# Thresholds on POOL in two batches, first-chunk casts on ACT, and one copy for the last columns of two tiles

## The chip, the cores and the metric

The kernel runs on one core of one Trainium2 chip. The metric is the device time of one execution in microseconds (us), the median of three runs. One execution was also taken by the hardware profiler; its trace is what the tables below are read from. The engines are PE (matrix multiply; PEld is its weight load), DVE (vector), ACT (activation, with function tables), POOL (GpSimd) and SP, which only issues DMAs here.

## What is computed

Eight batches of eight heads of attention over 576 positions of 64 values, with a threshold: a score counts only if it is at least the row's maximum minus tau. The result goes through a feed-forward layer with softplus.

```python
scores = scale * np.matmul(q, k.transpose(0, 1, 3, 2))
thresh = np.max(scores, axis=-1, keepdims=True) - tau
scores = np.where(scores >= thresh, scores, -1000000000.0)
attn = np.exp(scores - np.max(scores, axis=-1, keepdims=True))
attn = attn / (np.sum(attn, axis=-1, keepdims=True) + 1e-09)
attn_out = np.matmul(attn, v)
...
h = x @ w_in
g = np.maximum(h, 0.0) + np.log1p(np.exp(-np.abs(h)))
return (g @ w_out).astype(np.float32)
```

Here x is the attention output as 4608 rows of 512, w_in is 512 x 2048 and w_out 2048 x 512.

## The kernel before

**Attention.** Two heads of a batch form a unit; there are 32 units, four to a batch. A unit has nine tiles of 128 query rows: tiles 0 to 3 are of the first head, tiles 5 to 8 of the second, and tile 4 holds the last 64 rows of both. The 288 tiles run in order. For each tile, `scores` (L375) multiplies on PE into one of two PSUM banks (s_0, s_1), `row_max` (L395) takes the negated row maximum on DVE (L398, negm) and makes the threshold thr from it, `exps` (L405) takes the exponential on ACT (L406), and `mask` (L409) multiplies the exponentials by "score at least thr" on DVE (L411), which also gives the row sums. `weights_T` (L428) transposes the masked tile on PE in pieces of 128 columns (L444), and the last 64 columns of two neighbouring tiles together as one piece (L441); a tile 4 has a piece of its own (L447).

**Upper and lower parts.** PE multiplies in fp32r, a rounded form. So each operand is split into an upper part (a cast) and a lower part (the value minus its upper part). For the attention weights `weights_hi` (L468) copies the transposed pieces on ACT into gH (L464 in batch 0, where signs are turned, L466 elsewhere), and `weights_lo` (L476) makes the lower parts (by PE in batch 0, L485 and L487; by DVE elsewhere, L125). The lower parts of the last 64 columns (L497, L500 through L125) are put in the other 64 partitions of the same columns of gH. `values` (L502) multiplies with v and `values_out` (L515) puts the result into xp. `scale_x` (L550) scales xp on POOL by row factors that come back by DMA, and it goes to DRAM.

**The thresholds.** In batch 0 (the first TG = 36 tiles) thr is made by ACT (L400), in all later tiles by DVE (L402):

```python
nc.vector.reduce_max(negm, s.sp[t][:, :, 0:HS], axis=AX.XY, negate=True)
if 9 * NPAIR * s.b + 9 * s.hp + t < TG:
    nc.scalar.activation(thr, negm, AF.Identity, bias=ntau, scale=-1.0)
else:
    nc.vector.tensor_scalar(out=thr, in0=negm, scalar1=-1.0, scalar2=ntau, op0=ALU.mult, op1=ALU.add)
```

**Feed-forward.** Rows of x go in nine chunks of 512. `hidden` (L590) multiplies with w_in (L603, L605, L607), `softplus` (L618) runs on ACT over two PSUM banks at a time, with a load of its function table, and `parts_of` (L635) splits each result st: the upper part by DVE (L122, GV = 1), the lower by POOL (L125). `project` (L652) multiplies with w_out (L661 to L665). Chunk 0 starts at tile 41, in batch 1, and its matmuls are dealt out among the tiles.

**The weights.** The two weight matrices come as 64-bit words and are made into fp32 upper and lower parts while batches 0 and 1 run, in 32 pieces, one every two tiles: ACT (L176), POOL (L177), DVE three times (L181, L182, L184), POOL twice (L118, L125), and for w_in a store to DRAM and a load back.

**What sets the order.** The program is written out tile by tile by a loop over step letters (L888). A scheduler then places the instructions on each engine by the priority of their place in the program and by when it reckons them ready, so the order on an engine is not the written one, and it changes when a step moves to another engine. Each engine runs its instructions in the order it was given.

Of the kernel before, what the change touches and what calls it, by code (L numbers as in the profile page):

```python
# [12 lines left out]
AF = mybir.ActivationFunctionType  # L13
ALU = mybir.AluOpType
# [9 lines left out]
P = 128  # L24
# [26 lines left out]
GV = 1  # L51
TG = 36
W1 = 2.0
W0 = 1
SPA = 0


@with_exitstack
def tile_kernel(ctx: ExitStack, tc: tile.TileContext, q, k, v, tau, w_in, w_out, out):
# [8 lines left out]
    nc = tc.nc  # L68
# [6 lines left out]
    NC = SM // P  # L75
    NPAIR = H // 2
# [25 lines left out]
    ntau = cpool.tile([P, 1], F32, name="ntau")  # L102
# [4 lines left out]
                            op0=ALU.is_ge, op1=ALU.mult)  # L107
# [8 lines left out]
    def hi_of(eng, out_, in_):  # L116
        if eng is nc.gpsimd:
            eng.tensor_scalar(out=out_, in0=in_, scalar1=1.0, scalar2=1.0, op0=ALU.mult, op1=ALU.mult)  # L118
        elif eng is nc.scalar:
            eng.copy(out_, in_)  # L120
        else:
            eng.tensor_copy(out_, in_)  # L122

    def lo_of(eng, out_, in_, hi):
        eng.tensor_tensor(out=out_, in0=in_, in1=hi.bitcast(F32), op=ALU.subtract)  # L125
# [123 lines left out]
    for b in range(B):  # L249
        for kind in (("one", "two") if b < NSPLIT else ("all",)):  # L250
            for hp in range(NPAIR):
                s = Unit()
# [12 lines left out]
                s.cols = (slice(0, NC), slice(0, 2), slice(2, NC))[("all", "one", "two").index(kind)]  # L265
                s.eng = (nc.gpsimd, nc.scalar)[SPA] if b < NSPLIT else nc.gpsimd
                s.neg = 9 * NPAIR * b + 9 * hp < TG
# [127 lines left out]
    def row_max(s, t):  # L395
        negm = apool.tile([P, 1], F32, tag="negm", bufs=3, name=f"negm_{s.i}_{t}")
        thr = apool.tile([P, 1], F32, tag="thr", bufs=3, name=f"thr_{s.i}_{t}")
        nc.vector.reduce_max(negm, s.sp[t][:, :, 0:HS], axis=AX.XY, negate=True)  # L398
        if 9 * NPAIR * s.b + 9 * s.hp + t < TG:
            nc.scalar.activation(thr, negm, AF.Identity, bias=ntau, scale=-1.0)  # L400
        else:
            nc.vector.tensor_scalar(out=thr, in0=negm, scalar1=-1.0, scalar2=ntau, op0=ALU.mult, op1=ALU.add)  # L402
        s.m[t] = (negm, thr)
# [10 lines left out]
    def group(s, g):  # L414
        if g not in s.grp:
            h = apool.tile([P, NC + 1, 320], F32R, tag="gH", name=f"gH_{s.i}_{g}")
            l = apool.tile([P, NC, 320], F32R, tag="gL", name=f"gL_{s.i}_{g}")
            s.grp[g] = (h, l)
        return s.grp[g]

    def mate(s, t):

        if t == NC:
            return None, False
        u = t if t < NC else t - 1
        return (t + 1, False) if u % 2 == 0 else (t - 1, True)
# [23 lines left out]
    def rests(s, t):  # L450

        lo, hi = slice(0, SR), slice(SR, P)
        other, second = mate(s, t)
        if other is None:
            return [(t, lo, lo, hi)]
        if not second:
            return []
        return [(x, (lo, hi)[s.half[x]], (lo, hi)[s.half[x]], (hi, lo)[s.half[x]]) for x in (other, t)]
# [3 lines left out]
    def copy(s, out_, in_):  # L462
        if s.neg:
            nc.scalar.activation(out_, in_, AF.Copy, scale=-1.0)  # L464
        else:
            nc.scalar.copy(out_, in_)  # L466

    def weights_hi(s, t):  # L468
        main, rest = s.sp[t]
        for g, c0, s0, n in s.place[t]:  # L470
            copy(s, group(s, g)[0][:, 0:NC, c0:c0 + n], main[:, :, s0:s0 + n])
        for x, rows, up, _ in rests(s, t):
            for g, c0, s0, n in s.place[x]:
                copy(s, group(s, g)[0][up, NC, c0:c0 + n], rest[rows, s0:s0 + n])

# [142 lines left out]
    def softplus(u, full):  # L618


        ts, last_ = [], None
        with tc.high_priority(SPP):
            for fc, bank in reversed(full):
                t = fpool.tile([P, TC], F32, tag="st", bufs=NST, name=f"st_{u.n}_{fc}")
                i = nc.scalar.activation(t, bank, AF.Softplus).ins  # L625
                if last_ is not None:
                    tc.add_manual_dep(i, last_.name, mybir.DependencyInfo(
                        mybir.DependencyClass.NoSync, mybir.DependencyReason.DATA), reason="one table load")
                last_ = i
                ts.append((fc, t))  # L630
        defer(HD[1], lambda: [parts_of(u, fc, t) for fc, t in reversed(ts)])
# [3 lines left out]
    def parts_of(u, fc, t):  # L635

        pool, tags, bufs = (fpool, ("gh", "gl"), NG)
        if u.tail:
            spare = [("kT", 2), ("qT0", 2), ("qT1", 2), ("nat", 3), ("vt", 3)]
            i = later_g[0] % (NG + len(spare))  # L640
            later_g[0] += 1
            if i >= NG:
                tag, bufs = spare[i - NG]
                pool, tags = apool, (tag, tag)
        gh, gl = [pool.tile([P, TC], F32R, tag=tags[i], bufs=bufs, name=f"g{i}_{u.n}_{fc}") for i in range(2)]
        hi_of(nc.vector if GV else nc.scalar, gh, t)
        lo_of(nc.gpsimd, gl, t, gh)
        for i in range(TC // u.T):
            c = slice(i * u.T, (i + 1) * u.T)
            u.g[fc + i] = (gh[:, c], gl[:, c])  # L650
# [118 lines left out]
    while sum(u.T for u in chunks) < NT:  # L769
        u = Chunk()  # L770
# [24 lines left out]
    for kind, g in WL:  # L795
        for m in range(4):
            n = len(prep)
            prep.append((int(W0 + n * W1), prep_w_in if kind == "i" else prep_w_out,
                         (g, m) if kind == "i" else (4 * g + m,)))
# [72 lines left out]
    u0.eng, u0.eng_lo = eng, nc.gpsimd  # L872
    scores(*tiles[0])
    row_max(*tiles[0])
    exps(*tiles[0])
    scores(*tiles[1])
# [5 lines left out]
    for g, (cur, t) in enumerate(tiles):  # L882
# [5 lines left out]
        for step in PAT0 + ("m" if g == TG - 1 else "") if g < TG else PAT:  # L888
            if step == "T":
                weights_T(cur, t)  # L890
            elif step == "h":
                weights_hi(cur, t)
            elif step == "l":
                weights_lo(cur, t)
            elif step == "R" and nxt:
                row_max(*nxt)
            elif step == "e" and nxt:
                exps(*nxt)
            elif step == "m" and nxt:
                mask(*nxt)  # L900
            elif step == "M":
                mask(cur, t)
            elif step == "f":
                upto += quota / PAT.count("f")
                while done < upto:
                    done += next(ffn)
            elif step == "x":
                extras(cur.i, cur.tiles.index(t))
            elif step == "S" and g + 2 < NS:
                scores(*tiles[g + 2])  # L910
            elif step == "w":
                while prep and prep[0][0] <= g:
                    _, f, a = prep.pop(0)
                    f(*a)
            elif step == "p":
                point()
# [38 lines left out]
```

## Time and profile before

| what | value |
|---|---|
| median of three runs | 1489.3 us (1488.03 to 1491.64) |
| the profiled execution | 1491.63 us, of which the span from first to last instruction is 1489.6 us |
| PE | 1416.6 us busy, 95% of the span |
| PE weight load | 1195.5 us, 80% |
| DVE | 1019.5 us, 68% |
| ACT | 892.2 us, 60% |
| POOL | 600.3 us, 40% |
| mean granted clock of PE | 0.986 of full speed |

The page of the profile divides the span into 40 slices of some 37 us. In the first eight PE is busy for 6 to 9 tenths and the others for 4 to 9; from the ninth on PE shows 9 tenths, which here means 90% or more, in every slice but the last. Batch 0 runs to about 157 us, batch 1 to about 325 us. A busy PE is not PE at its peak, since matmuls are pipelined and their ends are modelled.

### The profile page before, as it was taken

Reading aid. Unit: us, or ns where it says so; the run is one execution under the profiler, and the core shown is the slowest. Engines: PE = TensorE matmul, PEld = TensorE weight load, DVE = VectorE, ACT = ScalarE, POOL = GpSimd, SP = SyncE. Lnnn points to the kernel's source line nnn. Section 1 sums busy time; section 2 is a strip of 40 time slices with the busy share of each in tenths; the row PEclk is TensorE's granted clock in tenths of the full one; section 3 lists DMA queues with packets and bytes.
Section 4 is the critical chain, followed back from the end, with each engine's and each line's share of the span. In section 5 each row is a group of like instructions: output and inputs, shape, how many; then the busy total and the mean of one; then the engine's idle time right before and its main releaser. Section 6 shows DMA issues by size and latency. Waiting matters only on the chain.

```text
span 1489.6 us, 23959 instructions
## 1 busy us (share of the span) xinstructions
PE 1416.6 (95%) x8024; PEld 1195.5 (80%) x8024; DVE 1019.5 (68%) x2267; ACT 892.2 (60%) x1783; POOL 600.3 (40%) x629
## 2 busy tenths in 40 slices
PE   6787789899999999999999999999999999999998
PEld 5777667678888888888888888888888888788887
DVE  6878889878777777777777777777777777411111
ACT  5887577556766576666666676667665666411110
POOL 4656565534433443344334443334334331323221
PEclk9999899999999999999999999999999999999999
DMA  6756576434443454335333544345333532343321
GB/s 182 195 152 185 145 218 176 132 99 140 129 119 116 118 157 113 96 103 151 110 106 111 150 118 118 108 133 150 113 111 101 153 99 82 96 148 112 122 92 43
DMA packets 131211, 189.96 MB, mean 128 GB/s; under 512 B 35312, under 2 KB 86800, under 8 KB 131088
## 3 DMA queue, kind: packets, MB, share of 16 engines
q1 hardware_dynamic: 131088, 188.43, 43.9%
q8 instruction: 64, 1.05, 0.3%
q14 instruction: 59, 0.48, 0.1%
HBM read 140.51 MB, written 27.41 MB: 113 GB/s over the span
## 4 chain that ended last, share of the span: by engine, by line
PE 66%; ACT 11%; DVE 10%; issue 5%; POOL 4%; DMA 3%; SPq 1%; POOLq 0%; ACTq 0%; DVEq 0%
PE s L392 8%; PE s L444 7%; PE o L665 7%; PE o L663 7%; PE o L661 6%; PE h L603 6%; PE h L605 6%; PE h L607 6%; PE pv L510 3%; PE pv L511 3%; ACT gH L466 3%; DVE e_all L411 2%; ACT L625 2%; ACT e_all L406 2%; ACT st L625 2%
## 5 line engine op out<-in xcount | busy, mean ns | idle before, releaser
L466 ACT CAST gH<-s 128x512 fp32r<-128x512 f32 (+3 forms) x560 | 207.7, 401 | 142.1 <-PE s L444 135.2
L125 POOL TENSOR_TENSOR g<-st,g 128x512 fp32r<-128x512 f32 x144 | 192.3, 1353 | 188.4 <-DVE g L122 188.4
L411 DVE SCALAR_TENSOR_TENSOR e_all<-s,thr,e_all 128x576 f32<-128x576 f32 x288 | 233.9, 815 | 39.0 <-ACT e_all L406 36.4
L398 DVE TENSOR_REDUCE negm<-s 128x1 f32<-128x576 f32 x288 | 217.2, 754 | 38.2 <-PE s L392 34.4
L665 PE MATMUL o<-wo_o,g 128*128 128x512 f32 x576 | 231.9, 403 | 5.6 <-POOL g L125 5.6
L605 PE MATMUL h<-xl,wi 128*128 128x512 f32 x576 | 233.9, 406 | 0.0
L661 PE MATMUL o<-wo_o,g 128*128 128x512 f32 x576 | 232.8, 404 | 0.0
L603 PE MATMUL h<-xh,wi 128*128 128x512 f32 x576 | 230.8, 401 | 1.5 <-ACT xh L120 0.9
L607 PE MATMUL h<-xh,wi 128*128 128x512 f32 x576 | 230.3, 400 | 0.0
L663 PE MATMUL o<-wo_o,g 128*128 128x512 f32 x576 | 228.6, 397 | 0.0
L406 ACT ACTIVATE e_all<-s,negm 128x576 f32<-128x576 f32 x288 | 214.0, 744 | 20.0 <-DVE negm L398 8.5
L125 DVE TENSOR_TENSOR gL<-s,gH 128x512 fp32r<-128x512 f32 (+1 forms) x280 | 175.0, 633 | 60.8 <-ACT gH L466 54.4
L392 PE MATMUL s<-kT,qT 128*128 128x288 f32 x1024 | 195.7, 313 | 7.9 <-DVE gH L125 3.6
L392 PEld LDWEIGHTS s<-kT,qT 128*128 128x128 f32 x1024 | 151.3, 193 | 25.8 <-DVE gH L125 15.7
L122 DVE CAST g<-st 128x512 fp32r<-128x512 f32 x144 | 67.6, 505 | 147.4 <-ACT st L625 146.7
L444 PE MATMUL s<-identr,e_all 128*128 128x128 f32 x1008 | 158.4, 280 | 9.4 <-DVE e_all L411 8.0
L625 ACT ACTIVATE st<-h 128x512 f32<-128x512 f32 x144 | 78.2, 596 | 118.3 <-PE h L607 117.7
L510 PE MATMUL pv<-gH,vt 128*128 128x320 f32 (+1 forms) x512 | 145.6, 304 | 1.8 <-ACT gH L466 1.8
L511 PE MATMUL pv<-gL,vt 128*128 128x320 f32 (+1 forms) x512 | 143.5, 301 | 0.5 <-DVE gL L125 0.5
L444 PEld LDWEIGHTS s<-identr,e_all 128*128 128x128 f32 x1008 | 114.2, 141 | 34.5 <-DVE e_all L411 30.3
L665 PEld LDWEIGHTS o<-wo_o,g 128*128 128x128 f32 x576 | 108.4, 188 | 30.1 <-POOL g L125 11.7
L603 PEld LDWEIGHTS h<-xh,wi 128*128 128x128 f32 x576 | 108.7, 189 | 24.7 <-ACT xh L120 1.2
(104 smaller groups left out, 2374.3 us busy)
## 6 DMA issues: line engine op xcount, KB each, us to landing
wi<-wi_d SPq DMA_DIRECT2D x144, 512.0 KB
qT<-qT SPq DMA_DIRECT2D x124, 128.0 KB
R<-r_d SPq DMA_DIRECT2D x64, 144.0 KB
kn<-in_k_dram SPq DMA_DIRECT2D x32, 256.0 KB
qn<-in_q_dram SPq DMA_DIRECT2D x32, 256.0 KB
vn<-in_v_dram SPq DMA_DIRECT2D x32, 256.0 KB
wc_i<-in_moe_w_in_dram SPq DMA_DIRECT2D x16, 512.0 KB
wi_d<-wc_i SPq DMA_DIRECT2D x32, 256.0 KB
```

The costliest lines, as they stand in the source:

```text
L125: eng.tensor_tensor(out=out_, in0=in_, in1=hi.bitcast(F32), op=ALU.subtract)
L392: nc.tensor.matmul(sp[:, hf, 0:HS], lhs, s.kT[j][:, k0 + hf * HS:k0 + (hf + 1) * HS], start=(m == 0), stop=(m == len(parts) - 1))
L406: nc.scalar.activation(e_all[:, s.half[t], :].rearrange("p (h n) -> p h n", h=2), s.sp[t][:, :, 0:HS], AF.Exp, bias=s.m[t][0], scale=1.0)
L411: nc.vector.scalar_tensor_tensor(out=e2, in0=s.sp[t][:, :, 0:HS], scalar=s.m.pop(t)[1], in1=e2, op0=ALU.is_ge, op1=ALU.mult, accum_out=s.s ...
L444: nc.tensor.matmul(main[:, c, :], e[:, c0:c0 + P], ident, is_transpose=True, start=True, stop=True)
L466: nc.scalar.copy(out_, in_)
L603: nc.tensor.matmul(h, wi[:, 0, cc, :], u.h[cc], start=(cc == 0), stop=False)
L605: nc.tensor.matmul(h, wi[:, 0, cc, :], u.l[cc], start=False, stop=False)
L607: nc.tensor.matmul(h, wi[:, 1, cc, :], u.h[cc], start=False, stop=(cc == NCC - 1))
L661: nc.tensor.matmul(o, gh[:, sl], wo[fc][:, 0, :], start=(i == 0), stop=False)
L663: nc.tensor.matmul(o, gh[:, sl], wo[fc][:, 1, :], start=False, stop=False)
L665: nc.tensor.matmul(o, gl[:, sl], wo[fc][:, 0, :], start=False, stop=(i == QF - 1))
```

## The change

Three edits. The thresholds of batches 0 and 1 (72 tiles) are made by POOL instead of ACT (batch 0) and DVE (batch 1); later batches keep DVE. The 16 upper parts of chunk 0's softplus results are cast by ACT instead of DVE; later chunks keep DVE. And where the last 64 columns of two neighbouring tiles stand in one transposed piece, one copy of 128 partitions x 256 replaces two copies of 64 partitions x 128: it writes the piece twice, side by side, and the half of each that doesn't belong there is written over by the lower parts, as before. There are four such pairs in a unit, 128 in all.

```diff
+TP = 2
...
-        if 9 * NPAIR * s.b + 9 * s.hp + t < TG:
-            nc.scalar.activation(thr, negm, AF.Identity, bias=ntau, scale=-1.0)
+        if s.b < TP:
+            nc.gpsimd.tensor_scalar(out=thr, in0=negm, scalar1=-1.0, scalar2=ntau, op0=ALU.mult, op1=ALU.add)
         else:
             nc.vector.tensor_scalar(out=thr, in0=negm, scalar1=-1.0, scalar2=ntau, op0=ALU.mult, op1=ALU.add)
...
-        for x, rows, up, _ in rests(s, t):
+        both = rests(s, t)
+        if len(both) == 2:
+
+            (g, c0, _, n), = s.place[both[0][0]]
+            copy(s, group(s, g)[0][:, NC, c0:c0 + 2 * n].rearrange("p (k n) -> p k n", k=2),
+                 rest.unsqueeze(1).to_broadcast([P, 2, n]))
+            return
+        for x, rows, up, _ in both:
...
-        hi_of(nc.vector if GV else nc.scalar, gh, t)
+        hi_of(nc.vector if u.n else nc.scalar, gh, t)
```

The edits also let the scheduler place other instructions differently in batches 0 and 1. In the rows below a name ends in a running number; negm_2_3_1179 is the row maximum of unit 2, tile 3, and wa_o1 is a piece of w_out on its way through the three DVE steps L181, L182 and L184. The line numbers of the changed kernel are higher by one (by eight from L476 on).

DVE in batch 0, from the row maximum of unit 2's tile 2 to its mask and the next, before:

```order
L398 TENSOR_REDUCE negm_2_2_1133<-s_0_137 128x1
L181 TENSOR_SCALAR wa_o1_1170<-wa_o1_1170 128x512
L182 SCALAR_TENSOR_TENSOR wa_o1_1170<-wc_o1_1169,wa_o1_1170 128x512
L522 TENSOR_TENSOR xp_1_766<-xp_1_766,pv_1_3_1116 64x256
L184 SCALAR_TENSOR_TENSOR wa_o1_1170<-wc_o1_1169,wa_o1_1170 128x512
L398 TENSOR_REDUCE negm_2_3_1179<-s_1_138 128x1
L497 SCALAR_TENSOR_TENSOR gH_2_0_1104<-tr_2_1_1139,gH_2_0_1104 64x128 x2
L411 SCALAR_TENSOR_TENSOR e_all_136,sums_2_1002<-s_0_137,thr_2_2_1134,e_all_136 128x576
L411 SCALAR_TENSOR_TENSOR e_all_136,sums_2_1002<-s_1_138,thr_2_3_1180,e_all_136 128x576
```

Before, seven instructions stand between the maximum and the mask of this tile, three of them steps of a weight piece. The same place in the changed kernel:

```order
L399 TENSOR_REDUCE negm_2_2_1125<-s_0_137 128x1
L412 SCALAR_TENSOR_TENSOR e_all_136,sums_2_995<-s_1_138,thr_2_1_1082,e_all_136 128x576
L530 TENSOR_TENSOR xp_1_761<-xp_1_761,pv_1_3_1108 64x256
L412 SCALAR_TENSOR_TENSOR e_all_136,sums_2_995<-s_0_137,thr_2_2_1126,e_all_136 128x576
L505 SCALAR_TENSOR_TENSOR gH_2_0_1096<-tr_2_1_1131,gH_2_0_1096 64x128 x2
L399 TENSOR_REDUCE negm_2_3_1170<-s_1_138 128x1
L182 TENSOR_SCALAR wa_o1_1161<-wa_o1_1161 128x512
L183 SCALAR_TENSOR_TENSOR wa_o1_1161<-wc_o1_1160,wa_o1_1161 128x512
L399 TENSOR_REDUCE negm_2_4_1218<-s_0_137 128x1
L185 SCALAR_TENSOR_TENSOR wa_o1_1161<-wc_o1_1160,wa_o1_1161 128x512
L412 SCALAR_TENSOR_TENSOR e_all_136,sums_2_995<-s_1_138,thr_2_3_1171,e_all_136 128x576
```

Now the mask of tile 2 stands ahead of the weight steps, of the lower parts (L505) and of the next maximum; the mask of tile 3 no longer follows at once. The five places of this kind in batch 0 are tiles 2 and 4 of unit 1, tiles 2 and 7 of unit 2 and tile 4 of unit 3.

POOL in batch 1, around the lower parts of chunk 0's softplus results (g1_0) and the weight pieces wc_i3, before:

```order
L125 TENSOR_TENSOR g1_0_3_2511<-st_0_3_2475,g0_0_3_2510 128x512
L177 TENSOR_SCALAR wa_i3_2_2473<-wa_i3_2_2473 128x512
L118 TENSOR_SCALAR wc_i3_2_2472<-wa_i3_2_2473 128x512
L125 TENSOR_TENSOR wc_i3_2_2472<-wa_i3_2_2473,wc_i3_2_2472 128x512
L125 TENSOR_TENSOR g1_0_4_2648<-st_0_4_2622,g0_0_4_2647 128x512
L125 TENSOR_TENSOR g1_0_5_2652<-st_0_5_2620,g0_0_5_2651 128x512
L177 TENSOR_SCALAR wa_i3_3_2587<-wa_i3_3_2587 128x512
L551 TENSOR_TENSOR xp_4_2062<-xp_4_2062,R_4_2538 128x576
```

And in the changed kernel:

```order
L126 TENSOR_TENSOR g1_0_3_2490<-st_0_3_2455,g0_0_3_2489 128x512
L119 TENSOR_SCALAR wc_i3_2_2452<-wa_i3_2_2453 128x512
L126 TENSOR_TENSOR wc_i3_2_2452<-wa_i3_2_2453,wc_i3_2_2452 128x512
L401 TENSOR_SCALAR thr_5_2_2469<-negm_5_2_2468,ntau_85 128x1
L178 TENSOR_SCALAR wa_i3_3_2566<-wa_i3_3_2566 128x512
L401 TENSOR_SCALAR thr_5_3_2528<-negm_5_3_2527,ntau_85 128x1
L126 TENSOR_TENSOR g1_0_4_2626<-st_0_4_2600,g0_0_4_2625 128x512
L559 TENSOR_TENSOR xp_4_2045<-xp_4_2045,R_4_2517 128x576
L126 TENSOR_TENSOR g1_0_5_2630<-st_0_5_2598,g0_0_5_2629 128x512
L178 TENSOR_SCALAR wa_o8_2692<-wa_o8_2692 128x512
L119 TENSOR_SCALAR wc_i3_3_2565<-wa_i3_3_2566 128x512
L126 TENSOR_TENSOR wc_i3_3_2565<-wa_i3_3_2566,wc_i3_3_2565 128x512
```

A threshold now stands behind whatever POOL has ahead of it: thr_5_2 behind the two steps of a weight piece, thr_5_4 (the next row after these) behind two more.

## Rows read from the trace of the kernel before

**Rows 1.** Stages: PE, PEld, DVE, ACT, POOL busy us (instructions), granted clock, DMA.

```profile
10.00:160.00 150.00, 117.55 (x757) 104.00 (x755) 120.69 (x239) 112.88 (x270) 88.75 (x104) 0.91 0.65 183
160.00:325.00 165.00, 147.67 (x825) 120.35 (x824) 137.36 (x295) 107.07 (x207) 92.07 (x101) 0.96 0.54 156
325.00:1260.00 935.00, 924.90 (x5440) 788.24 (x5440) 704.28 (x1617) 620.78 (x1215) 352.83 (x367) 1.00 0.42 119
```

**Rows 2.** Waits of PE, 10 to 160 us: us in total, times, longest.

```profile
PE tm L444 <- DVE e_all L411: 21.5, 13, 3.3
PE tl L487 <- ACT gH L464: 4.3, 11, 1.6
...
PE tr L441 <- DVE e_all L411: 1.8, 5, 0.8
```

**Rows 3.** Waits of PE, 160 to 325 us.

```profile
PE s L392 <- DVE gL L125: 4.2, 3, 2.3
PE s L444 <- DVE e_all L411: 4.1, 6, 1.0
PE s L392 <- DVE gH L125: 3.6, 2, 3.2
PE s L441 <- DVE e_all L411: 1.8, 2, 1.6
```

**Rows 4.** Timeline of PE, DVE and ACT: start, us, instruction, [idle before, releaser].

```profile
60.12 0.63 PE L444 MATMUL tm<-identr,e_all 128*128 128x128 f32 x4 [1.92 <-DVE e_all L411]
...
87.42 1.50 DVE L181 TENSOR_SCALAR wa_o<-wa_o 128x512 uint32<-128x512 uint32 x1 [0.25 <-POOL wa_o L177]
...
88.29 0.74 ACT L406 ACTIVATE e_all<-s,negm 128x576 f32<-128x576 f32 x1
...
92.47 0.82 DVE L411 SCALAR_TENSOR_TENSOR e_all<-s,thr,e_all 128x576 f32<-128x576 f32 x1
...
93.45 1.09 PE L444 MATMUL tm<-identr,e_all 128*128 128x128 f32 x4 [2.88 <-DVE e_all L411]
...
136.81 1.08 PE L444 MATMUL tm<-identr,e_all 128*128 128x128 f32 x4 [2.80 <-DVE e_all L411]
```

**Rows 5.** Two stretches after such a wait: busy us as in rows 1, granted clock.

```profile
92.70:99.30 6.60, 5.85 (x26) 5.77 (x27) 3.81 (x8) 2.09 (x5) 1.21 (x3) 0.50 0.49 126
...
137.00:140.30 3.30, 3.30 (x17) 3.25 (x17) 2.93 (x3) 0.86 (x4) 1.68 (x2) 0.51 0.16 39
```

**Rows 6.** Groups by line and form: count, busy us, mean ns of one, idle before.

```profile
L466 ACT CAST gH<-s 64x128 fp32r<-64x128 f32 x224 | 58.1, 260 | 2.4
...
L120 ACT CAST xh<-xst 128x512 fp32r<-128x512 f32 x36 | 21.6, 620 | 20.4 <-PE h L607 11.7 <-DMA xst<-x_d 8.7
...
L466 ACT CAST gH<-s 128x256 fp32r<-128x256 f32 x56 | 18.6, 396 | 2.5 <-PE s L447 2.4
...
L118 POOL TENSOR_SCALAR q<-qn 128x256 fp32r<-128x256 f32 x31 | 12.9, 418 | 25.8 <-PE tr L333 25.2
...
L400 ACT ACTIVATE thr<-negm,ntau 128x1 f32<-128x1 f32 x36 | 10.8, 300 | 1.5 <-DVE negm L398 1.3
```

**Rows 7.** DVE's casts of line L122, 160 to 325 us: busy us, count.

```profile
160.00:325.00 165.00, 8.53 (x14) 0.96 0.54 156
```

**Rows 8.** DVE's thresholds of line L402, 160 to 325 us: busy us, count.

```profile
160.00:325.00 165.00, 6.80 (x33) 0.96 0.54 156
```

**Rows 9.** Timeline of POOL and DVE at a mask in batch 1, two places.

```profile
157.69 0.87 POOL L125 TENSOR_TENSOR q<-qn,q 128x320 fp32r<-128x320 f32 x1
...
158.11 0.82 DVE L411 SCALAR_TENSOR_TENSOR e_all<-s,thr,e_all 128x576 f32<-128x576 f32 x1
...
272.88 0.81 DVE L411 SCALAR_TENSOR_TENSOR e_all<-s,thr,e_all 128x576 f32<-128x576 f32 x1
272.93 0.88 POOL L125 TENSOR_TENSOR vt<-vn,vt 128x320 fp32r<-128x320 f32 x1
```

**Rows 10.** Line L181, all instructions of it on w_in pieces: ns min/median/max, first and last start.

```profile
L181 DVE TENSOR_SCALAR wa_i<-wa_i x16: 409/427/1632, 16.8 to 218.0; 128x512 uint32<-128x512 uint32 x16
```

## The prediction

> **What bounds the kernel now.** I read the busy time by stage first, because the shares over the whole span mix two kinds of work. In batch 0 (10 to 160 us) PE is busy for 117.55 of 150 us and idle for 32.5; in batch 1 (160 to 325 us) it is idle for 17.3; in the 935 us after that for only 10.1 [rows 1]. So what this change can win lies almost wholly in the first 325 us, and what it does to ACT after that can win at most a part of 10.1 us. PE's order is fixed and the later work is full, so a microsecond won early is won at the end.
>
> Next I asked what PE waits for. In batch 0, 21.5 of its 32.5 idle us end with a mask of DVE at L444, in 13 waits, 1.8 in five more at L441, and 4.3 with a copy of ACT [rows 2]. In batch 1 the largest waits all end with DVE too: 4.2 and 3.6 for lower parts, 4.1 and 1.8 for masks, in 8 tiles of 36 [rows 3]. DVE is busy for 120.69 of 150 and 137.36 of 165 us, ACT for 112.88 and 107.07, POOL for 88.75 and 92.07 [rows 1]. No engine is full, so it is latency and the order on DVE that count.
>
> Last I looked at one such wait closely. The exponential of tile 2 of unit 2 ends on ACT at 88.29 + 0.74 = 89.03. Its mask starts on DVE at 92.47, 3.4 us later, since DVE runs the steps of a weight piece first, beginning with L181 at 87.42; PE waits for it for 2.88 us [rows 4]. The threshold was long there. So ACT's thresholds are not what PE waits for: what matters is where the masks stand on DVE.
>
> **The change, part by part.** The sum is made against the profiled execution, 1491.6 us; the median of the runs shown, 1489.3, is 2.3 less, and I take that off at the end.
>
> *Masks moved forward on DVE in batch 0.* The order of the changed kernel puts five masks ahead of weight steps, of lower parts and of the next maximum. In the trace the PE waits at these five places are 1.92, 1.62, 2.88, 1.92 and 2.80 us, in all 11.1; the first, the third and the last stand in [rows 4]. At most all of it goes: -11.1. At least nothing does, because the next maximum and so the next mask move back by what was put ahead of them. DVE does the same work in batch 0 as before, so I take the middle: **-5.5**.
>
> *ACT in batch 0.* It loses 36 thresholds of 300 ns, 10.8 us, and 16 pairs of copies of 260 ns each become one of about 396 ns, as a copy of 128x256 takes [rows 6]: 16 x 124 ns = 2.0. The 12.8 us are 11% of 112.88. I let PE's waits for ACT, 4.3 us, shrink by that share: **-0.5** (between 0 and -4.3).
>
> *The clock.* After the long waits PE's granted clock falls. In the 6.6 us from 92.7, behind the wait of 2.88, it is 0.50 of full speed, which is the lower level, 1.2 GHz; behind the wait of 2.80 it is 0.51 over 3.3 us [rows 4, 5]. In these two stretches PE is busy for 5.85 + 3.30 = 9.15 us, half of which, 4.6, would go at 2.4 GHz. If the waits get shorter, some of these falls don't come; I take half: **-2.3** (between 0 and -4.6; new waits could bring new ones).
>
> *DVE in batch 1.* It loses 14 casts in this stage, 8.53 us [rows 7], and 33 thresholds, 6.80 us [rows 8], together 11% of its 137.36. PE's four largest groups of waits for DVE sum to 13.7 us [rows 3]. A cast or threshold taken out shortens such a wait only if it stands in the unbroken run of DVE instructions that ends in the awaited one, so I take their share of DVE's work and not more: 11% of 13.7, **-1.5** (between 0 and -13.7).
>
> *Thresholds behind other work on POOL.* A POOL step of 256 columns takes 418 ns, and DVE's threshold of one column 0.21 us [rows 6, 8]; for the new step I take 0.25 us with its hand-over. For all 72 tiles I set the row maximum's end and the end of what POOL has ahead of the threshold, both at the times of the trace, against the start of the mask. In batch 0 one threshold would be late, by 0.05 us. In batch 1 nine would be, by 10.5 us in all. The first is the mask at 158.11, while POOL is busy until 157.69 + 0.87 = 158.56; the last the one at 272.88, against 272.93 + 0.88 = 273.81 [rows 9]. A late threshold stops DVE, which runs in order, and whatever stands behind the mask. PE waited for masks in 8 of 36 tiles there, so I charge 0.22 of it: **+2.3** (between 0 and +10.5).
>
> Here the Trainium skill speaks against the move. DVE's step L181 takes 427 ns at the median and up to 1632 [rows 10], and the one of 1.50 us falls in a stretch where POOL works too [rows 4]. Perfetto Trace Analysis, section Optimizing Scalar/DVE Operations, says that POOL reads SBUF through a port that DVE shares, so that moving work between these two may not help. If every fourth of the 72 thresholds waited out half a DVE step of 0.8 us, they would be late by 7 us more; at the same share as above that is 1.6 us, and the sum below would be 1.6 us higher. The spread of L181 agrees with the rule; no row shows it for a step of one column.
>
> *ACT in batch 1.* It gains 14 casts of 620 ns [rows 6], 8.7 us, and loses 16 x 124 ns; 6.7 us on 107.07 [rows 1]. The upper parts now come from the engine that made the results, so no hand-over is added, and none of PE's largest waits there is for ACT [rows 3]. I take **+0.5** (between 0 and the whole 6.7), nearest to the rows that show no wait.
>
> *After batch 1.* 96 pairs save 96 x 124 ns = 11.9 us of ACT, which is busy for 620.78 of 935 us there, while PE is idle for 10.1 in all: **0** (between -1 and +1).
>
> The sum: -5.5 - 0.5 - 2.3 - 1.5 + 2.3 + 0.5 = -7.0, so 1484.6 for a run like the profiled one and **1482.3** at the median. A measurement of this kernel can tell a difference of about 0.3%, 4.5 us, from none.
>
> **Rivals.**
> - *Larger.* The five waits go whole and the clock stays up behind them: -11.1 - 4.6 - 1.5 = -17.2, or 1472.1. For it: the exponentials are ready 2 to 3 us before these masks. Against it: DVE's work in batch 0 is unchanged, and the maxima are moved back.
> - *No difference.* Moving masks forward only passes the lateness on to the next tile. Then batch 0 gives -0.5, batch 1 -1.5 + 2.3 + 0.5 = +1.3, and the time is 1490.1. For it: masks that stood in pairs now stand apart, with a maximum and weight steps between them.
> - *Slower.* POOL's queue becomes what the masks wait for. The place is a threshold that stands behind a weight piece (L118, L125) or a lower part of 1.3 us, as thr_5_2 does. If thresholds in batch 0 come as late as I find for batch 1, 10.5 us over 36 tiles or 0.29 us each, then, with PE waiting for masks at 18 places in 36 tiles [rows 2], half of it counts, +5.3, and nothing is won by the masks or the clock: 5.3 - 0.5 + 1.3 = +6.1, or 1495.4. It decides from there on, about 0.3 us a tile in batch 0; 0.05 us in one tile is what the times of before give.
> - *The edits not done as written.* The scheduler could have kept the two copies or the masks where they were; the order rows show that it didn't, so I give it no chance of its own.
>
> **How the numbers follow.** The forecast has 0.46, larger 0.16, no difference 0.24, slower 0.14. Nearly all of the forecast's own spread (1478 to 1486) is a gain of over 0.3%, which is below 1484.8: faster 0.59; the rest of it and the second rival make same 0.27; slower 0.14. The range reaches from a little below the larger rival to the slower one, 1470 to 1495.
>
> **What would show it.** PE's waits for L444 after a mask in batch 0 fall from 21.5 to some 14 us, and the two stretches at the lower clock get fewer. DVE's busy time in batch 1 falls by about 15 us. Batch 0 should end some 8 us earlier, batch 1 about 7, and the stage after it should be as long as before. The copies of 128x256 should take about 396 ns, and POOL's thresholds 0.2 to 0.4 us. The forecast is wrong if masks wait for POOL by more than a few us in batch 0, if the last mask of batch 1 is not earlier than 325 - 4 us, or if the stage after it changes by more than 2 us.

## The result, and the profile after

The changed kernel takes 1493.3 us (median of 22 executions, 1491.6 to 1497.1) against 1490.3 us of the kernel before measured beside it (22 executions, 1488.0 to 1494.7): a ratio of 1.0018, 95% interval 1.0011 to 1.0025. It is slower by 0.18%, less than the 0.3% that I called a difference, and 11 us above the forecast. The profiled execution of the changed kernel took 1492.1 us, that of the kernel before 1491.6.

The stages of the changed kernel, in the columns of [rows 1]:

```profile
10.00:160.00 150.00, 113.63 (x751) 101.33 (x749) 117.84 (x233) 102.33 (x217) 101.53 (x142) 0.93 0.65 181
160.00:325.00 165.00, 145.58 (x799) 119.43 (x799) 120.90 (x243) 107.74 (x201) 104.38 (x135) 0.94 0.54 158
325.00:1260.00 935.00, 924.24 (x5463) 792.96 (x5464) 707.48 (x1623) 604.87 (x1129) 353.00 (x368) 1.00 0.42 119
```

Batch 0 is the first line, batch 1 the second. The relief that I had counted is there: ACT loses 10.6 us of work in batch 0, DVE 16.5 in batch 1. POOL gains 12.8 and 12.3. But PE gets through fewer instructions in the time of batch 1, 799 where it was 825. The start of a tile's mask on DVE tells where the time goes. Tile 36, the first of batch 1, is 0.5 us later than before, tile 72, the first of batch 2, 4.6 later, and the last tile 0.2. So batch 1 loses 4.1 us, and the later stage, from which I expected nothing, wins 4.4.

PE's waits in batch 0 (10 to 160 us), which answer to [rows 2]:

```profile
PE tm L445 <- DVE e_all L412: 17.8, 10, 3.6
PE tr L442 <- DVE e_all L412: 4.7, 4, 1.8
PE tl L495 <- ACT gH L465: 4.5, 9, 1.6
```

and in batch 1 (160 to 325 us), which answer to [rows 3]:

```profile
PE s L442 <- DVE e_all L412: 6.7, 6, 3.7
PE pv L519 <- DVE gL L126: 3.9, 2, 3.3
PE s L393 <- DVE gH L126: 3.3, 1, 3.3
PE rT L542 <- DVE rs L538: 1.8, 1, 1.8
```

In batch 0 the two kinds of wait for masks sum to 22.5 us; before they summed to 23.3. They have only moved, as PE's timeline shows:

```profile
95.87 0.43 PE L442 MATMUL tr<-identr,e_all 128*128 128x128 f32 x1 [1.82 <-DVE e_all L412]
...
119.17 0.63 PE L445 MATMUL tm<-identr,e_all 128*128 128x128 f32 x4 [2.48 <-DVE e_all L412]
128.40 0.63 PE L445 MATMUL tm<-identr,e_all 128*128 128x128 f32 x4 [2.43 <-DVE e_all L412]
140.35 1.09 PE L445 MATMUL tm<-identr,e_all 128*128 128x128 f32 x4 [3.03 <-DVE e_all L412]
```

The wait of 2.88 at 93.45 [rows 4] is gone, and others have taken its place. PE's waits of 1.5 us and more in batch 0 sum to 19.8 us before and 20.1 after, nine each time.

The costs of single instructions came out near what I took (groups by line and form; thr is the new threshold on POOL):

```profile
L467 ACT CAST gH<-s 128x256 fp32r<-128x256 f32 x168 | 61.2, 386 | 2.2 <-PE s L448 2.1
L401 POOL TENSOR_SCALAR thr<-negm,ntau 128x1 f32<-128x1 f32 x72 | 27.8, 387 | 40.0 <-DVE negm L399 34.8 <-DVE rs L537 2.5 <-DMA vn<-in_v_dram 1.0
L121 ACT CAST g<-st 128x512 fp32r<-128x512 f32 x16 | 9.6, 623 | 0.0
```

What I had not counted stands behind the second bar of the second line: POOL sat idle for 34.8 us at the head of its queue, waiting for row maxima of DVE. And DVE waits for POOL. These are its waits in batch 1 (160 to 325 us) that end with POOL:

```profile
DVE wa_o L182 <- POOL wa_o L178: 7.3, 5, 4.9
DVE wa_i L182 <- POOL wa_i L178: 6.2, 3, 3.2
DVE e_all L412 <- POOL thr L401: 3.1, 6, 0.9
DVE ws_o L182 <- POOL ws_o L178: 1.5, 1, 1.5
```

Only 3.1 us are masks that wait for thresholds. 15.0 us are weight steps (L182) that wait for POOL's step on the same piece (L178). Before, these waits summed to 8.1:

```profile
DVE wa_i L181 <- POOL wa_i L177: 4.1, 3, 2.4
DVE wa_o L181 <- POOL wa_o L177: 2.9, 3, 1.1
DVE ws_o L181 <- POOL ws_o L177: 1.1, 1, 1.1
```

### The profile page after: what moved, and what is told of

Read it like the earlier page. It is cut to its first block, busy times and chain, and to the rows that moved or that the text cites. A ratio compares the mean times of both kernels' runs of the same rounds, so it can differ in the third digit from the quotient of the medians.

```text
span 1489.8 us, 23934 instructions
## 1 busy us (share of the span) xinstructions
PE 1410.5 (95%) x8024; PEld 1197.6 (80%) x8024; DVE 1003.6 (67%) x2215; ACT 866.5 (58%) x1635; POOL 625.5 (42%) x701
## 4 chain that ended last, share of the span: by engine, by line
PE 74%; DVE 7%; ACT 5%; POOL 4%; issue 3%; DMA 1%; SPq 0%; POOLq 0%; DVEq 0%; ACTq 0%
PE s L393 10%; PE h L613 8%; PE h L611 8%; PE h L615 8%; PE o L673 7%; PE o L671 7%; PE o L669 7%; PE s L445 7%; PE pv L519 4%; PE pv L518 4%; DVE e_all L412 2%; PE tr L334 2%; POOL g L126 2%; DVE negm L399 1%; ACT L633 1%
## 5 line engine op out<-in xcount | busy, mean ns | idle before, releaser
L467 ACT CAST gH<-s 128x512 fp32r<-128x512 f32 (+1 forms) x448 | 186.6, 467 | 144.2 <-PE s L445 141.3
L123 DVE CAST g<-st 128x512 fp32r<-128x512 f32 x128 | 58.9, 497 | 149.5 <-ACT st L633 149.0
L445 PEld LDWEIGHTS s<-identr,e_all 128*128 128x128 f32 x1008 | 116.3, 142 | 21.3 <-DVE e_all L412 12.6
```

Source lines behind the costliest of these rows:

```text
L445: nc.tensor.matmul(main[:, c, :], e[:, c0:c0 + P], ident, is_transpose=True, start=True, stop=True)
```

## The experiments

Three theories stood at the start. **A**: thresholds on POOL tie two in-order queues together, which costs more than the masks win, and the pair copies win something that I missed. **B**: the casts on ACT cost more than the 0.5 us that I gave them. **C**: the order that the scheduler finds shifts batches 0 and 1 by some us whatever is edited.

### One edit at a time

e1_pairs_only is the kernel before with the third edit alone.

```diff
+        both = rests(s, t)
+        if len(both) == 2:
...
+            copy(s, group(s, g)[0][:, NC, c0:c0 + 2 * n].rearrange("p (k n) -> p k n", k=2),
+                 rest.unsqueeze(1).to_broadcast([P, 2, n]))
+            return
...
```

> The one copy for the last columns of two tiles, alone. Theory A (this copy is what made the later part of the changed kernel faster: there the mask of tile 287 made up 4.4 us on the mask of tile 72, 0.020 us a tile): the same 0.020 us a tile from tile 72 on, so 4 us by the last mask, and batches 0 and 1 within 2 us of before, in all 3 to 6 us faster. Rival (the later part made up time because batch 1 had left work behind, not because of the copy): no gain from tile 72 on, in all within 2 us of before.

Measured: 1479.6 us, ratio 0.9932 (0.9915 to 0.9949). That is more than either theory gave. In the profiled execution the mask of tile 72 comes 8.2 us earlier than before, and that of the last tile 13.7: most of the gain lies in batches 0 and 1.

e2_thresholds_only has the first edit alone.

```diff
+TP = 2
...
+        if s.b < TP:
+            nc.gpsimd.tensor_scalar(out=thr, in0=negm, scalar1=-1.0, scalar2=ntau, op0=ALU.mult, op1=ALU.add)
...
```

> The thresholds of batches 0 and 1 on POOL, alone. Theory A (thresholds tie POOL's queue to DVE: they wait there for row maxima, hold the weight steps behind them, and DVE's weight steps and masks wait in turn): 4 to 8 us slower, lost in batch 1, with DVE's waits for POOL in 160 to 325 us at 14 us or more where before they sum to 8.1. Rival B (the casts on ACT lost the time): within 2 us of before, and the waits as before.

Measured: 1498.2 us, ratio 1.0047 (1.0034 to 1.0061). The size is what theory A gave, the place and the wait are not. In the profiled execution 4.3 us are lost ahead of the mask of tile 36, in batch 0, and 2.8 in batch 1. DVE's waits for POOL in 160 to 325 us sum to 12.4 us, of which 5.2 are masks that wait for thresholds and 7.2 weight steps, no more than before.

e3_casts_only has the second edit alone.

```diff
-        hi_of(nc.vector if GV else nc.scalar, gh, t)
+        hi_of(nc.vector if u.n else nc.scalar, gh, t)
```

> Chunk 0's casts on ACT, alone. Theory A: within 2 us of before, since DVE gets 8 us of work less in batch 1 and ACT 9 us more and neither is full. Rival B (the casts hold up exponentials and copies on ACT): 3 to 6 us slower, lost in batch 1, with DVE's wait of gL for ACT's gH in 160 to 325 us at 8 us or more where before it is 6.2.

Measured: 1496.0 us, ratio 1.0038 (1.0024 to 1.0051).

e4_pairs_thr_batch0 is the change without its casts, and with POOL's thresholds in batch 0 only.

```diff
-TP = 2
+TP = 1
...
-        hi_of(nc.vector if u.n else nc.scalar, gh, t)
+        hi_of(nc.vector if GV else nc.scalar, gh, t)
```

> The one copy, and POOL's thresholds in batch 0 alone; batch 1 keeps DVE's thresholds and casts. Theory A: batch 0 within 1 us of before at the mask of tile 36, no loss in batch 1, and the copy's gain, so 3 to 6 us faster than before. Rival C (any change of the order in batches 0 and 1 shifts them by some us, up or down, with no rule): anywhere from 8 us faster to 3 us slower, with batch 1 changed by more than 2 us.

Measured: 1484.9 us, ratio 0.9960 (0.9947 to 0.9974), as theory A said.

So one edit wins 11.0 us and the two others lose 7.6 and 5.5 by themselves. I had the only winner at next to nothing. Of e3's loss most falls between the masks of tiles 72 and 90 (2.7 of 3.2 us at the last tile, in its profiled execution), behind batch 1, where neither theory put it. The granted clock of that stretch is 0.98, against 1.00 before; which wait makes the loss I did not follow.

### Where the pair copy wins

Between the masks of tile 72 and of the last tile e1 gains 5.5 us, some 0.025 us a tile (a little more in the first 36), in a stage where PE shows 10.1 us of idle time [rows 1] and hardly a wait. The engine to ask there is PEld. Its waits from 325 to 1260 us, in the kernel before:

```profile
PEld s L444 <- DVE e_all L411: 21.4, 70, 0.7
PEld s L392 <- DVE gH L125: 10.0, 36, 0.6
PEld o L665 <- POOL g L125: 9.9, 12, 0.9
```

and in e1_pairs_only:

```profile
PEld s L444 <- DVE e_all L411: 10.3, 26, 0.7
PEld o L672 <- POOL g L125: 9.9, 12, 0.9
PEld s L392 <- issue: 8.7, 29, 0.3
PEld s L392 <- DVE gL L125: 2.3, 7, 0.3
PEld s L441 <- DVE e_all L411: 2.3, 8, 0.4
PEld s L392 <- ACT gH L466: 2.2, 6, 0.4
```

All waits of the weight loads there sum to 48.1 us before and 37.8 in e1 ("issue" is time in which nothing that the trace shows was waited for). The waits for masks halve: L444 and L441 together have 24.0 us before and 12.6 in e1. The weight loads of the next scores (L392) wait no less, 11.4 us and then 13.2; only what ended last before them is another. PE's row hardly shows any of this: in these 935 us it is busy for 924.90 us with 5440 instructions before, and for 925.69 with 5470 in e1. So what was won lies inside its "busy" time.

e5_pairs_late uses the pair copy from batch 2 on, with batches 0 and 1 in their old order:

```diff
-        if len(both) == 2:
+        if len(both) == 2 and s.b >= 2:
```

> The pair copy only from batch 2 on; batches 0 and 1 keep the two copies and their order of before. Theory A (after batch 1 PE's work is stretched by its weight loads' waits for masks, 21.4 us before and 10.3 with the pair copy, and the pair copy gives 0.025 us a tile there): the mask of tile 72 within 0.5 us of before, that of tile 287 earlier by 5 to 6 us, ratio about 0.996. Rival C (the gain after batch 1 needs the earlier start or the other order of batches 0 and 1): no gain after tile 72, within 1 us, ratio about 1.000.

Measured: 1484.9 us, ratio 0.9964 (0.9952 to 0.9976). The mask of tile 72 comes 1.0 us earlier, that of the last tile 7.0: 6.0 won in between, with the order ahead of it untouched. The weight loads' waits for masks at L444 are 10.3 us, as in e1. So the pair copy itself wins this, and it is not an effect of the reordering in batches 0 and 1.

e6_pairs_extra puts ACT time back, by a copy whose result nothing uses, from batch 2 on:

```diff
+    extra = cpool.tile([SR, 16], F32, tag="extra", name="extra")
...
+        if len(both) == 2:
...
+            if s.b >= 2:
+                nc.scalar.copy(extra, group(s, g)[0][both[0][2], NC, c0:c0 + 16].bitcast(F32))
...
```

> The pair copy everywhere, and from batch 2 on one more ACT copy of 64x16 behind each (its result is not used), which mostly stands behind the next exponential. Theory S2 (what counts is the time from the transposes to the next exponential and mask, not ACT's total time): the gain after tile 72 stays, 4 to 6 us, ratio about 0.993. Rival S1 (what counts is ACT's load: 124 ns saved a pair, some 200 ns put back): the gain after tile 72 goes, between 0 and a loss of 4 us, ratio about 0.997 to 1.000.

Measured: 1484.4 us, ratio 0.9962 (0.9948 to 0.9976). The extra copy takes 201 ns, more than a pair saves (2 x 260 - 386 = 134). Still 3.5 us of the gain after tile 72 stay: a little under what S2 gave, and the wrong sign for S1. The time follows the weight loads' waits for masks. From the mask of tile 90 to that of the last tile it is 876.4 us before, 872.8 in e6 and 871.5 in e1, with 24.0, 15.1 and 12.6 us of such waits from 325 us on. So behind batch 1 it counts mostly when the next masks can start, and not ACT's load. The whole kernel speaks less clearly: by its median e6 is 4.9 us above the pair copy alone (e9), and its ratio is nearer to S1's. In its profiled execution the last mask comes 6.8 us later than in e1's, and 4.7 of them are lost ahead of tile 72, where no extra copy runs; why is open.

e9_pairs_again is e1's kernel once more, since e6's batch 0 had ended 2.8 us later with the same order there.

```diff
+        both = rests(s, t)
+        if len(both) == 2:
...
```

> The pair copy alone once more, since e6_pairs_extra, which has the same order through batch 0, showed batch 0 ending 2.8 us later than e1_pairs_only did. Theory A (the pair copy wins about 5.5 us before tile 72 and 5.5 behind it): median 1478 to 1482, ratio about 0.993. Rival D (the early part of the first result was the luck of that kernel's executions; only the part behind tile 72 is real): 1484 to 1486, ratio about 0.9965.

Measured: 1479.5 us, ratio 0.9920 (0.9907 to 0.9933). The early half of the gain, 5.4 us between e5 and e1, is real too. Which wait of batches 0 and 1 it comes from I did not settle; batch 0 of e6's profiled execution is 2.8 us longer than that of e1's.

### Where the thresholds and the casts lose

e7_pairs_thr is the change without its casts:

```diff
-        hi_of(nc.vector if u.n else nc.scalar, gh, t)
+        hi_of(nc.vector if GV else nc.scalar, gh, t)
```

> The change without its casts: pair copies, thresholds of batches 0 and 1 on POOL. If the costs add (pairs -11.0, thresholds +7.6): -3.4, 1487.2, ratio about 0.998, and the casts are worth +5 in the change. If the thresholds are the whole loss of the change (Theory A alone, casts cost nothing): as the change itself, 1493, ratio about 1.002. Rival B (casts are the larger part): below 1485, ratio under 0.996.

Measured: 1484.4 us, ratio 0.9958 (0.9945 to 0.9970). This speaks for B: in the change the casts are worth 9.0 us.

e8_spare_thr is the kernel before, and POOL makes each threshold of batches 0 and 1 a second time for nothing:

```diff
+        if s.b < 2:
+            spare = apool.tile([P, 1], F32, tag="spare", bufs=2, name=f"spare_{s.i}_{t}")
+            nc.gpsimd.tensor_scalar(out=spare, in0=negm, scalar1=-1.0, scalar2=ntau, op0=ALU.mult, op1=ALU.add)
```

> The kernel before, and in batches 0 and 1 POOL makes each threshold a second time into a tile that nothing reads: POOL's queue waits for the row maximum as in the change, but no mask waits for POOL. Theory A1 (the loss comes through POOL's queue: it stands at the head for a maximum, weight steps and lower parts behind it come late): most of the 7.6 us, +4 to +8, ratio about 1.004. Rival A2 (the loss comes from masks that wait for POOL's threshold): within 1.5 us of before, ratio about 1.000.

Measured: 1491.5 us, ratio 1.0011 (1.0002 to 1.0020). That is 1.4 us, as A2 has it. POOL waits for maxima here too, 24.4 us between 10 and 325 us against 30.0 in the change, and by itself this costs little. That the loss of e2 comes from those who wait for POOL's thresholds fits this, but this kernel's order is another one too, and no run holds the order fixed.

e10_pairs_casts has the pair copies and the casts, without POOL's thresholds:

```diff
+        if len(both) == 2:
...
-        hi_of(nc.vector if GV else nc.scalar, gh, t)
+        hi_of(nc.vector if u.n else nc.scalar, gh, t)
```

> Pair copies and chunk 0's casts on ACT, thresholds as before. The casts cost 5.5 us alone and the change is 9.0 above the kernel with pair copies and thresholds. Theory B1 (the casts delay ACT's own copies and exponentials in batch 1, whoever makes the thresholds): 5 to 9 us above the pair copy alone, 1485 to 1489, ratio about 0.998. Rival B2 (they cost only where POOL's thresholds tie DVE and POOL together in batch 1): within 2 us of the pair copy alone, about 1480, ratio 0.993.

Measured: 1480.6 us, ratio 0.9933 (0.9920 to 0.9947): 1.2 us above the pair copies alone, so B2 and not B1.

e11_pairs_thr0_casts is the change with POOL's thresholds in batch 0 only:

```diff
-TP = 2
+TP = 1
```

> The change with POOL's thresholds in batch 0 only; e4_pairs_thr_batch0 (1484.9) is the same without the casts. Theory B1 (casts cost by themselves): 1490 to 1494, 5 to 9 us above that, ratio 1.000 to 1.002. Rival B2 (only together with thresholds on POOL in batch 1): within 2 us of 1485, ratio about 0.9965.

Measured: 1484.6 us, ratio 0.9951 (0.9938 to 0.9964), again B2. (Its profiled execution was the longest of five, 1490.5 us, mostly by a late end of batch 0.)

Four of these kernels make a square, all with pair copies and with POOL's thresholds in batch 0:

| | casts on DVE | casts on ACT |
|---|---|---|
| batch 1's thresholds on DVE | 1484.9 (e4) | 1484.6 (e11) |
| batch 1's thresholds on POOL | 1484.4 (e7) | 1493.3 (the change) |

Each edit is free by itself here; together they cost 9 us. The loss lies in batch 1: from the mask of tile 36 to that of tile 72 the change takes 179.4 us in its profiled execution, e7 172.1, e4 173.7 and e11 174.5. C, which would let any edit of the order cost some us, doesn't give such a square easily: three corners agree within 0.5 us. It is not excluded, since the order differs in every corner and the change's may be the one unlucky one. Without the casts, DVE's waits for POOL in batch 1 are (e7, whose profiled execution was its fastest, 1481.5 us):

```profile
DVE wa_o L182 <- POOL wa_o L178: 3.4, 5, 1.4
DVE wa_i L182 <- POOL wa_i L178: 1.2, 1, 1.2
DVE e_all L412 <- POOL thr L401: 1.1, 3, 0.8
...
DVE ws_o L182 <- POOL ws_o L178: 0.5, 1, 0.5
```

In the change the first two have grown from 4.6 to 13.5 us. The longest of these waits came about like this. POOL, in the changed kernel:

```profile
263.36 0.64 POOL L401 TENSOR_SCALAR thr<-negm,ntau 128x1 f32<-128x1 f32 x1 [2.91 <-DVE negm L399]
...
268.88 2.51 POOL L126 TENSOR_TENSOR g<-st,g 128x512 fp32r<-128x512 f32 x2
271.38 0.27 POOL L401 TENSOR_SCALAR thr<-negm,ntau 128x1 f32<-128x1 f32 x1
271.73 0.61 POOL L178 TENSOR_SCALAR wa_o<-wa_o 128x512 f32<-128x512 f32 x1
```

and what it does to DVE and PE:

```profile
272.38 0.43 DVE L182 TENSOR_SCALAR wa_o<-wa_o 128x512 uint32<-128x512 uint32 x1 [4.86 <-POOL wa_o L178]
272.72 0.75 DVE L126 TENSOR_TENSOR gL<-s,gH 128x256 fp32r<-128x256 f32 x2
...
273.19 0.44 PE L519 MATMUL pv<-gL,vt 128*128 128x320 f32 x1 [3.32 <-DVE gL L126]
```

A threshold holds POOL's queue for 2.91 us until its maximum is there. From then on POOL works with one pause of 0.34 us, but a weight piece, a scaling, a pair of q's parts, the lower parts of two softplus results (2.51 us) and one more threshold stand ahead of L178, the short step that DVE needs. L182 stands at the head of DVE's queue and waits for it for 4.86 us. Behind it are the lower parts gL that PE's next matmul needs. In the same way L182 waits 3.19 us at 201.87 and 1.99 at 209.86, and PE waits 3.71 for the mask behind the latter.

e10, in which DVE makes the thresholds, has the first two of these waits too (3.20 and 4.28 us; PE waits 1.96 and 2.98 behind them), so the casts bring them about. It gets away with them, and so does e11, whose waits of this kind in batch 1 sum to 14.3 us, nearly as many as the change's 15.0:

```profile
DVE wa_o L182 <- POOL wa_o L178: 8.0, 4, 4.1
DVE wa_i L182 <- POOL wa_i L178: 6.0, 3, 3.2
...
DVE ws_o L182 <- POOL ws_o L178: 0.3, 1, 0.3
```

So DVE's waits for weight steps are not what the 9 us consist of. PE's waits of 1 us and more between 160 and 330 us sum to 15.0 in the change, 12.4 in e4, 11.3 in e11, 10.3 in e10 and 4.3 in e7. What the change has more of than all of them is PE's waits for masks: 7.1 us between 160 and 325 us, against 4.1 in e4, 2.2 in e7, 1.8 in e11 and 1.5 in e10. The longest of these is the 3.71 behind a weight step above. That batch 1's thresholds on POOL make the masks late behind such steps fits this; it is argued from these waits and not shown.

Two more kernels ask whether POOL's queue is the cause, or only this one order. e13_lower_on_dve is the change with chunk 0's lower parts on DVE:

```diff
-        lo_of(nc.gpsimd, gl, t, gh)
+        lo_of(nc.gpsimd if u.n else nc.vector, gl, t, gh)
```

> The change, with the lower parts of chunk 0's softplus results made by DVE instead of POOL: 16 x 1.29 us leave POOL's queue in batch 1, 16 x some 0.7 us come to DVE, which the change had relieved of about that much. Theory E (in the change POOL's queue in batch 1 is too long: these lower parts and the thresholds that wait for a maximum stand ahead of the weight steps L178, and DVE waits for those at the head of its own queue, 15.0 us against 5.1 in e7_pairs_thr): the 9 us come back, 1482 to 1487, ratio 0.995 to 0.998, DVE's waits for L178 in batch 1 below 8 us. Rival F (the 9 us are this one order of instructions, not POOL's load): 1490 to 1496.

e14_clamp_on_dve is the change with POOL's step L178 of the later weight pieces on DVE:

```diff
-            nc.gpsimd.tensor_scalar(out=m, in0=m, scalar1=W_MAX, scalar2=W_MIN, op0=ALU.min, op1=ALU.max)
+            pieces[0] += 1
+            eng = nc.vector if pieces[0] > 16 else nc.gpsimd
+            eng.tensor_scalar(out=m, in0=m, scalar1=W_MAX, scalar2=W_MIN, op0=ALU.min, op1=ALU.max)
...
+    pieces = [0]
```

> The change, with step L178 of the later half of the weight pieces made by DVE instead of POOL, so that DVE waits for ACT there and no longer for POOL; some 16 x 0.43 us more on DVE. Theory E: those waits of DVE for POOL go, most of the 9 us come back, 1483 to 1488, ratio 0.995 to 0.9985. Rival F: 1490 to 1496.

Measured: e13 1485.0 us, ratio 0.9953 (0.9941 to 0.9966); e14 1485.1 us, ratio 0.9968 (0.9957 to 0.9979). In both, some 8 of the 9 us come back, though DVE gets more work. DVE's waits for POOL's weight steps fall to 5.0 us in e13:

```profile
DVE e_all L412 <- POOL thr L401: 5.0, 7, 1.3
DVE wa_o L182 <- POOL wa_o L178: 2.8, 2, 1.7
...
DVE wa_i L182 <- POOL wa_i L178: 1.2, 1, 1.2
DVE ws_o L182 <- POOL ws_o L178: 1.0, 1, 1.0
```

In e14 there are none. Masks still wait for thresholds, 5.0 us in e13 and 3.2 in e14, and that doesn't hurt. Both came out in the range that E gave, by different ways of relieving POOL's queue, and F gave 1490 or more for each; batch 1 takes 173.4 us in e13 and 173.7 in e14 where it took 179.4. So less work in POOL's queue is enough to get rid of the loss. But F is not quite refuted: each of the two has another order as well, and if only the change's own order were unlucky, both would also come out near 1485. And of E's mechanism the part about DVE's waits for L178 doesn't stand: e14 has none of them and e11 has 14.3 us, and both take 1485 us.

### A better version

e12_pairs_thr_dve has pair copies, and the thresholds of batch 0 on DVE (the edit against e1):

```diff
-            nc.scalar.activation(thr, negm, AF.Identity, bias=ntau, scale=-1.0)
+            nc.vector.tensor_scalar(out=thr, in0=negm, scalar1=-1.0, scalar2=ntau, op0=ALU.mult, op1=ALU.add)
```

> Pair copies, and the thresholds of batch 0 by DVE, as in all later batches: no hand-over between maximum, threshold and mask, 36 more instructions of 0.21 us on DVE (7.5 us) and 36 fewer of 0.30 on ACT. If hand-overs are what thresholds elsewhere cost: faster than the pair copy alone by 1 to 3 us, 1477 to 1479, ratio 0.992. If DVE's load decides in batch 0: slower by 2 to 7 us, 1482 to 1487, ratio 0.995 to 0.998.

Measured: 1480.2 us, ratio 0.9927 (0.9915 to 0.9938): neither of the two outcomes, within a microsecond of the pair copies alone. The version that beats both kernels is the pair copy alone, at 1479.5 us, 0.7 to 0.8% below the kernel before. POOL's thresholds in batch 0 cost 5 us on top of it (e4 against e1), 3.5 of them in batch 0 and 3.9 in batch 1 in the profiled executions; of this loss I know the size and not the chain.

## Why the prediction was wrong

- **"What it does to ACT after that can win at most a part of 10.1 us", and the term "after batch 1: 0".** This is one of the two steps that failed. The change wins 4.4 us there, e5 6.0. The saving in ACT time was sized well (the copy takes 386 ns, I took 396), but I took PE's idle time as the bound, and 48.1 us of waits stood on PEld, 24.0 of them for masks. The Trainium skill warns of this bound, in Perfetto Trace Analysis, section Identifying the Most-Contended Engine: the busy share of PE's matmuls is not a good measure of how close a kernel is to roofline, and the arithmetic rate reached and the busy share of the weight loads are to be used instead. The trace agrees: PEld is busy for 788 of the 935 us [rows 1] where PE shows 925, and there were 4 to 6 us to win.
- **Masks moved forward: "-5.5".** It failed whole. The waits at the five places went and came back at others (23.3 to 22.5 us). The reason that I gave for the lower end, that maxima and so the next masks move back, fits these waits, and I took the middle all the same. My rival "no difference" said this of batch 0: -0.5 forecast, +0.5 measured at the mask of tile 36.
- **ACT in batch 0: "-0.5", and the clock: "-2.3".** ACT lost 10.6 us of work and PE's waits for ACT's gH went from 4.3 to 4.5: nothing. The granted clock did rise in batch 0, from 0.91 to 0.93, and PE was busy for 113.63 us with 751 instructions where it had been busy for 117.55 with 757. But its idle time in these 150 us grew from 32.5 to 36.4, and batch 0 ended 0.5 us later. In batch 1 the clock fell, from 0.96 to 0.94.
- **DVE in batch 1: "-1.5".** DVE lost 16.5 us of work, where I said about 15, and waited more: for POOL's weight steps 15.0 us instead of 8.1, and 3.1 for thresholds.
- **Thresholds behind other work on POOL: "+2.3".** In batch 1 the term by itself is nothing (e7 against e4, -0.5 us); in batch 0, where I had 0.05 us, POOL's thresholds cost 5 us (e4 against e1). I set only the masks against POOL's queue (10.5 us late by my reckoning, 3.1 measured in batch 1). I didn't ask what stands behind a threshold that waits on POOL: 13.6 us of such waits for maxima in batch 1, with weight steps and lower parts behind them.
- **ACT in batch 1: "+0.5".** This is the other step that failed. "No hand-over is added" is true of the casts and leaves out POOL, whose lower parts follow them. In the change this term is worth 9.0 us, alone 5.5 (mostly behind batch 1), on top of the pair copies 1.2. The terms don't add up, and I priced each as if they did. That the 9.0 us need both the casts and batch 1's thresholds on POOL, and lie mostly in batch 1, is measured; by which chain they come about stays open.
- **The rivals.** The slower one named POOL's queue behind weight pieces and lower parts of 1.3 us, and gave 1495.4. It was nearest to what happened in batch 1, but decided by masks in batch 0, where POOL's thresholds come late 4 times for 3.7 us, and it missed the gain behind batch 1 as the forecast did. Both ways to a faster kernel, the forecast's and that of the larger rival, went through PE's waits for masks in batch 0, which stayed. The gain that I had left out and the losses that I had priced too low nearly cancel against the time before, so the time is inside the range by luck.
- **The signs of being wrong.** Two of the three that I named came: the last mask of batch 1 starts at 330.4 us, where it was to be earlier than 321, and the stage after it changed by 4.4 us and not by less than 2.

## What to carry to other kernels

Where PE looks full, read the waits of its weight loads before calling a saving worthless: here they waited 48 us where PE showed 10 us of idle time, and one copy less on ACT for each pair of tiles won 0.36% there (e5). When a step moves onto another engine's in-order queue, price both directions: who waits for it, and what stands behind it while it waits for its input. When two edits touch the same pair of queues, run the square of both: each was free here, and together they cost 9 us. And before a sum of waits is called the loss, look at it in a kernel without the loss: e11 has nearly the same waits of DVE for POOL as the change and is 8.8 us faster.

## What was not expected of the hardware

POOL's one-column threshold takes 260 to 280 ns in 46 of 72 cases and 0.31 to 1.01 us in the other 26 (two of the short ones stand in the timeline as one row of 0.51). Beside each of the 26 a weight step of DVE (L182, L183 or L185) runs, and beside none of the short ones; masks, row maxima and lower parts alone beside it don't matter. One of each:

```profile
131.58 0.63 POOL L401 TENSOR_SCALAR thr<-negm,ntau 128x1 f32<-128x1 f32 x1 [2.57 <-DVE negm L399]
...
131.40 0.68 DVE L185 SCALAR_TENSOR_TENSOR wa_i<-wc_i,wa_i 128x512 uint32<-128x512 uint32 x1
...
112.31 0.27 POOL L401 TENSOR_SCALAR thr<-negm,ntau 128x1 f32<-128x1 f32 x1 [1.04 <-DMA vn<-in_v_dram]
...
112.12 0.81 DVE L412 SCALAR_TENSOR_TENSOR e_all<-s,thr,e_all 128x576 f32<-128x576 f32 x1
```

The first threshold ends 0.13 us after DVE's step does; 24 of the 26 end 0.12 to 0.14 us after one. In sum the 72 take 8.4 us longer than 72 x 0.27. The rule of the Trainium skill that the prediction weighs (Perfetto Trace Analysis, section Optimizing Scalar/DVE Operations: POOL and DVE share a port for reading SBUF) fits this. My own estimate from it, 7 us of lateness, came out near in sum, though with 18 thresholds of 0.4 us each where 26 of 0.3 were measured. The trace adds that the long ones are those beside DVE's weight steps, whose operands all lie in SBUF, and not those beside its masks, which also read PSUM. What these 8.4 us cost the kernel no run here shows.
